# Pooled attention and a GELU MLP on one core: q transposed by DMA, loads reordered, matmuls on zeros added

## The chip, the core and the metric

The kernel runs on one core of a Trainium2 chip. The core has a matrix engine (TensorE, PE in the profile; its weight loads are PEld), a vector engine (VectorE, DVE), an activation engine (ScalarE, ACT), a general engine (GpSimd, POOL) and a queue processor (SyncE, SP). DMAs are issued from SP, ACT or POOL and run on 16 shared DMA engines. PSUM, where matmuls write, has 8 banks of 512 float32 columns on 128 partitions. The metric is the device time of one execution in microseconds (us), as the median of several runs.

## What is computed

Cut to what matters, for q, k and v of shape (8 batches, 8 heads, 576, 64):

```python
k_p = k.reshape(B, H, 72, 8, D).mean(axis=3)      # pooling by 8
v_p = v.reshape(B, H, 72, 8, D).mean(axis=3)
scores = np.matmul(q, k_p.transpose(0, 1, 3, 2)) / np.sqrt(D)
attn = softmax(scores)                            # over the 72 pooled keys
x = np.matmul(attn, v_p)                          # then (B*S, H*D) = (4608, 512)
h = x @ w_in                                      # (4608, 2048)
out = gelu_tanh(h) @ w_out                        # (4608, 512)
```

Inputs and output are float32; the kernel rounds to bfloat16 for the matmuls.

## The kernel before

**Two interleaved streams.** The MLP works through the 4608 tokens in 9 groups of 512 (`GROUP`). Attention works through 8 batches of 576 tokens. Batch 0 is done alone at the start; then group g of the MLP carries the attention of batch g + 1 between its own matmuls. The program order on each engine is written out by hand.

**One batch of attention.** `load_k`, `load_v` and `load_q` bring in float32 rows (q is cast to bfloat16 on the way[...]). k is pooled by three additions on VectorE (`k_steps`, line 135 through `add`), then turned by 5 TensorE transposes (`trans_k`, L162) and copied to `kT` (L168 to L172). v is pooled the same way (`v_steps`), into `vp` (for batch 0 into `vz`). q is turned by 18 TensorE transposes of 128x128 (`trans_q`, L179) into PSUM and copied to `qT` (L184 on ScalarE, L186 on VectorE), in four portions of 5 and 4 blocks (`QG`). Then there are 8 items (2 halves of the columns, 4 head pairs). Per item: `qk` makes two score matmuls (L196), `expo` one exponential (L202), `av` the product with v and the row sums (L215, for batch 0 four matmuls, L220), `norm` the reciprocal of the sums by a logarithm and an exponential on ScalarE (L228 to L233), and `mult` the product on VectorE into `xT` (L241), two instructions of 64 partitions, for batch 0 one of 128.

**One MLP group.** Phase 1: 16 blocks `fo` of 4 matmuls each (`p1_mm`, L266), each block followed by `gelu` on ScalarE (L272). The first four blocks are interleaved, the last `ko` of them last, as they need the latest `xT`. After each block the steps in `side[fo]` are issued, filled from `plan`: the pooling and the transposes of the next batch. Phase 2: 64 matmuls (`p2_mm`, L275); before matmul number `pos` = 6, 14, 20, ... the next batch's `qk`, `av`, `expo` and `norm` are issued, and `mult` some nine matmuls later. Four times per group a finished PSUM bank is copied (L280) and stored from the SP queue (L286).

**Banks.** Phase 1 uses PSUM banks 0 to 3 and 7. `trans_q` uses banks 4 to 7, one per portion, `trans_k` bank 4.

**Queues.** On SP: half of k of batch 0, v of batch 0 in two halves, v of batch 1, later the stores. On ACT: the rest of k of batch 0. On GpSimd: q of batch 0, the four quarters of `w_in`, k and q of batch 1, the four quarters of `w_out`, then at the head of each group g the k, q and v of batch g + 2. These buffers are double, so a load waits until the batch two earlier has been pooled or transposed.

**The start.** After batch 0's k is pooled: two portions of `trans_q`, `trans_k`, two portions of `trans_q`, eight times scores and exponential, `v_steps`, then the eight items of `av`, `norm` and `mult`. 16 matmuls of group 0 on the first 288 columns (`early`) are placed behind items 5, 6 and 7 (`take`). In group 0 the plan is: pooling of v at blocks 1 and 2, of k at block 7, q at 8 to 11, k's transposes at 13. In later groups: k pooled at 2 and 3, q at 4 to 7, k's transposes at 9, v at 10 to 13.

Of the kernel before, what the change touches and what calls it, by code (L numbers as in the profile page):

```python
# [8 lines left out]
F32 = mybir.dt.float32  # L9
BF16 = mybir.dt.bfloat16  # L10
ALU = mybir.AluOpType
# [7 lines left out]
def kernel(  # L19
# [9 lines left out]
    nc = tc.nc  # L29
    B, H, S, D = q.shape  # L30
    Sp = S // 8
# [6 lines left out]
    TP = T // 2  # L38
    CH = S // 2
# [33 lines left out]
    def load_v(b, eng, h0=0, h1=H):  # L73
        if b not in vs:
            vs[b] = kvp.tile([Sp, H, 512], F32, name="vt")
        eng.dma_start(out=vs[b][:, h0:h1],
                      in_=v[b, h0:h1].rearrange("h (j l) d -> j h (l d)", l=8))

    def load_q(b, i0=0, i1=2):
        if b not in qs:  # L80
            qs[b] = qp.tile([128, 2, T * D], BF16, name="qb")
        nc.gpsimd.dma_start(
            out=qs[b][:, i0:i1],
            in_=q[b].rearrange("(i h) (p t) d -> (h p) i (t d)", i=2, t=T)[:, i0:i1])
# [8 lines left out]
    load_k(0, [nc.sync, nc.scalar])  # L93
    load_v(0, nc.sync, 0, 4)
    load_v(0, nc.sync, 4, 8)
    load_v(1, nc.sync)
    load_q(0, 0, 1)
    load_q(0, 1, 2)
    make_identity(nc, identb)
    for i in range(4):  # L100
        nc.gpsimd.dma_start(out=w_in_b[:, :, i * 512:(i + 1) * 512], in_=w_in_v[:, :, i * 512:(i + 1) * 512])


    xT = consts.tile([128, KO, N], BF16, name="xT")
# [5 lines left out]

    vz = consts.tile([Sp, PR, 2, 2, D], BF16, name="vz")
    ones = consts.tile([Sp, 2, 2, D], BF16, name="ones")
    nc.vector.memset(kts[0][0:64, KR], 0.0)
    nc.vector.memset(kps[0], 0.0)
    nc.vector.memset(kTs[0], 0.0)
# [9 lines left out]

    load_k(1, [nc.gpsimd])
    load_q(1)
    for i in range(4):
        nc.gpsimd.dma_start(out=w_out_b[:, 4 * i:4 * i + 4, :], in_=w_out_v[:, 4 * i:4 * i + 4, :])

# [24 lines left out]
    def half_bank(bank):  # L155
        return PS[:, bank, :].bitcast(BF16)

    def trans_k(b, bank, odd_eng=None):
        tp = half_bank(bank)[:, 0:(KR + 1) * 128].rearrange("p (r c) -> p r c", c=128)
        kf = kps[b % 2].rearrange("p r d -> p (r d)")  # L160
        for r in range(KR + 1):
            nc.tensor.transpose(out=tp[:, r, :], in_=kf[:, r * D:r * D + 128], identity=identb)  # L162
        tp = tp[0:D]
        n7 = (H - 1) * KH
        for e in range(2):
            copy = nc.scalar.copy if e and odd_eng is nc.scalar else nc.vector.tensor_copy
            o = kTs[b % 2][e * 64:(e + 1) * 64, e]
            copy(out=o[:, 0:H - 1].rearrange("p h (j r) -> p h j r", r=KR),  # L168
                 in_=tp[:, 0:KR, 0:n7].rearrange("p r (h j) -> p h j r", j=KH))
            copy(out=o[:, H - 1, 0:(128 - n7) * KR].rearrange("p (j r) -> p j r", r=KR),  # L170
                 in_=tp[:, 0:KR, n7:128].rearrange("p r j -> p j r"))
            copy(out=o[:, H - 1, (128 - n7) * KR:], in_=tp[:, KR, 64:128])  # L172

    def trans_q(b, i, t0, n, bank, eng):
        if b not in qTs:
            qTs[b] = bp.tile([128, 2, 4, 32, TP], BF16, name="qT")
        tp = half_bank(bank)[:, 0:n * 128].rearrange("p (t h c) -> p h c t", h=4, c=32)
        for x in range(n):
            nc.tensor.transpose(out=half_bank(bank)[:, x * 128:(x + 1) * 128],  # L179
                                in_=qs[b][:, i, (t0 + x) * 128:(t0 + x + 1) * 128],  # L180
                                identity=identb)
        o = qTs[b][:, i, :, :, t0:t0 + n]
        if eng is nc.scalar:
            nc.scalar.copy(out=o, in_=tp)  # L184
        else:
            nc.vector.tensor_copy(out=o, in_=tp)  # L186

    QG = [(0, 0, 5), (0, 5, 4), (1, 0, 5), (1, 5, 4)]

# [3 lines left out]
    def qk(b, c, pr, bank):  # L193
        for e in range(2):
            h = 2 * pr + e
            nc.tensor.matmul(out=PS[:Sp, bank + e, :CH], lhsT=kTs[b % 2][:, c, h, :],  # L196
                             rhs=qTs[b][:, h // 4, h % 4].rearrange("p c t -> p (c t)"),
                             start=True, stop=True)

    def expo(b, c, pr, bank):  # L200
# [35 lines left out]
    def mult(b, c, pr, bank):  # L236
        rc = rcs.pop((b, c, pr))
        col = b * S + c * CH
        for x in range(2 if b else 1):
            rows = slice(x * 64, (x + 1) * 64) if b else slice(0, 128)  # L240
            nc.vector.tensor_tensor(out=xT[rows, pr, col:col + CH], in0=PS[rows, bank + x, :CH],  # L241
                                    in1=rc[rows], op=ALU.mult)

    ORDER = [(c, pr) for c in range(2) for pr in range(PR)]

# [47 lines left out]
    for s in k_steps(0):  # L293
        s()

    def scores(b, c, pr, bank):
        qk(b, c, pr, bank)
        expo(b, c, pr, bank)

    trans_q(0, *QG[0], 5, nc.scalar)  # L300
    trans_q(0, *QG[1], 6, nc.scalar)
    trans_k(0, 4, nc.scalar)
    trans_q(0, *QG[2], 5, nc.vector)
    trans_q(0, *QG[3], 6, nc.vector)
    for i, (c, pr) in enumerate(((0, 0), (0, 1), (1, 0), (1, 1), (0, 2), (0, 3), (1, 2), (1, 3))):
        scores(0, c, pr, (2, 0)[i % 2])
    for hf in range(2):
        for s in v_steps(0, hf):
# [4 lines left out]
    for i, (c, pr) in enumerate(ORDER):  # L313
        bank = (4, 6, 0, 2, 4, 6, 4, 6)[i]
        av(0, c, pr, bank)
        norm(0, c, pr, bank)
        mult(0, c, pr, bank)
        for fo, ko in early[:take[i]]:
            p1_mm(0, fo, ko, 0, CH)
        early = early[take[i]:]  # L320


    for g in range(NG):
        nb = g + 1 if g + 1 < B else None
        act_set(GELU_SET)
        if g + 2 < B:
            load_k(g + 2, [nc.gpsimd])
            load_q(g + 2)
            load_v(g + 2, nc.gpsimd)


        side = {fo: [] for fo in range(FO)}
        if nb is not None:
            kk = k_steps(nb)
            v0, v1 = v_steps(nb, 0), v_steps(nb, 1)
            tq = [lambda a=a, i=i: trans_q(nb, *a, 4 + i, nc.vector) for i, a in enumerate(QG)]
            tk = [lambda: trans_k(nb, 4)]
            if g:
                plan = {2: kk[:1], 3: kk[1:], 4: tq[:1], 5: tq[1:2], 6: tq[2:3], 7: tq[3:],
                        9: tk, 10: v0[:1], 11: v0[1:], 12: v1[:1], 13: v1[1:]}  # L340
            else:
                plan = {1: v0, 2: v1, 7: kk, 8: tq[:1], 9: tq[1:2], 10: tq[2:3], 11: tq[3:], 13: tk}
            for fo, what in plan.items():
                side[fo] += what

        if g == 0:
            first = [(fo, ko, CH) for ko in range(KO) for fo in range(4)]
        else:  # L350
            late = 3
            rest = [fo for fo in range(4) if fo != late]
            first = [(fo, ko, 0) for ko in range(2) for fo in rest]
            first += [(late, 0, 0), (late, 1, 0)]
            first += [(fo, ko, 0) for ko in (2, 3) for fo in rest + [late]]
        for fo, ko, c0 in first:
            p1_mm(g, fo, ko, c0)
        for fo in range(FO):
            if fo >= 4:
                for ko in range(KO):  # L360
                    p1_mm(g, fo, ko)
            gelu(g, fo)
            for s in side[fo]:
                s()


        todo = {}

        def at(m, f, *a):
            todo.setdefault(m, []).append((f, a))  # L370

        if nb is not None:
            act_set(EXP_SET)
            pos = (6, 14, 20, 27, 34, 41, 48, 55, 61)
            for i in range(len(ORDER) + 1):
                if i < len(ORDER):
                    at(pos[i], qk, nb, *ORDER[i], 2)
                if i:
                    a = (nb, *ORDER[i - 1], 4 + 2 * ((i - 1) % 2))
                    at(pos[i], av, *a)  # L380
                if i < len(ORDER):
                    at(pos[i], expo, nb, *ORDER[i], 2)
                if i:
                    at(pos[i], norm, *a)
                    at(min(pos[i] + 9, 65), mult, *a)
        seq = [(r, fo) for r in range(4) for fo in range(FO)]
        if g == 0:

            seq[:32] = [(r, 4 * f4 + f) for f4 in range(4) for r in range(2) for f in range(4)]
        for m, (r, fo) in enumerate(seq):  # L390
            for f, a in todo.pop(m, []):
                f(*a)
            p2_mm(g, r, fo)
            if fo == FO - 1:
                store(g, r)
        for m in sorted(todo):
            for f, a in todo[m]:
                f(*a)
# [30 lines left out]
```

The softmax here doesn't subtract the row's maximum and nothing guards it: scores larger than these inputs give would overflow.

## Time and profile before

| | |
|---|---|
| median of 5 runs | 320.72 us (319.49 to 322.3) |
| the profiled execution | 319.49 us, of which the span of its instructions is 317.5 us |
| VectorE busy | 176.0 us in 326 instructions |
| ScalarE busy | 222.2 us in 414 instructions |
| L179, q's transposes | 144 instructions, mean 231 ns each |
| L186, copies of q | 15 of 640 columns (mean 820 ns), 15 of 512 (mean 715 ns) |
| L241, `mult`, 64x288 | 112 instructions, mean 455 ns |
| L202, exponential | 64 instructions, mean 643 ns |
| L272, gelu | 144 instructions, mean 602 ns |
| DMA, first 76 us | about 0.25 MB per us |

How to read it: a busy time is the sum over the instructions of an engine. Matmuls overlap each other in the array, so the mean of one is its latency, and what one costs in a row of them is the distance from start to start. "Idle before" is the time in which the engine stood still ahead of an instruction, with what ended it. The chain is followed back from the last instruction through whatever released each step. Two further lines of times are needed below: on VectorE, batch 0's last product (L241) ran from 28.29 to 28.75 us, and the pooling of batch 1's k takes 2.34 us (two additions) and 0.49 us (the third). The `w_in` quarters took a median of 20.6 us from issue to landing, the `w_out` quarters 21.0 us.

### The profile page before, as it was taken

To read this page: it belongs to the slowest core of one execution; us is meant where nothing else is said; L and a number is where in the kernel's file an instruction comes from. 1 tells how busy PE (TensorE), PEld (TensorE's weight loads), DVE (VectorE), ACT (ScalarE), POOL (GpSimd) and SP (SyncE) were. 2 spreads that over 40 slices of the span, in tenths; PEclk is the share of its full clock that TensorE was granted. 3 is DMA by queue.
4 is the path that set the end of the run, shared out by engine and by line. 5 is a ranking of instruction groups with operands and counts; after the bars stand their busy time and mean duration, and the time that the engine had idled before them with its cause. 6 is when DMAs were issued, how large, how long until landed. Compare 5 with 4: busy or idle time off the path is not lost.

```text
span 317.5 us, 4296 instructions
## 1 busy us (share of the span) xinstructions
PE 303.3 (96%) x1624; PEld 156.6 (49%) x1624; DVE 176.0 (55%) x326; ACT 222.2 (70%) x414; POOL 29.5 (9%) x48
## 2 busy tenths in 40 slices
PE   0799999999999999999999999999999999999995
PEld 0556555454555455545554554555555544444442
DVE  2855926677568844984687467755775560010011
ACT  1595679866996789768986898679867987405600
POOL 8512320021002000101011100000000000000000
PEclk9999999999999999999999999999999999999999
DMA  7999999896813562275418440001200210021021
GB/s 230 261 257 263 226 271 208 254 247 160 206 44 132 124 157 94 51 210 125 122 35 223 104 146 34 0 18 51 66 2 0 66 68 0 26 76 34 0 66 66
DMA packets 17113, 37.50 MB, mean 118 GB/s; under 512 B 2021, under 2 KB 6117, under 8 KB 16197
## 3 DMA queue, kind: packets, MB, share of 16 engines
q0 software_dynamic: 10160, 24.26, 33.1%
q1 hardware_dynamic: 6708, 12.32, 12.0%
q10 hardware_dynamic: 224, 0.66, 0.6%
q8 instruction: 12, 0.20, 0.2%
q14 instruction: 9, 0.07, 0.1%
HBM read 36.70 MB, written 9.44 MB: 145 GB/s over the span
## 4 chain that ended last, share of the span: by engine, by line
PE 94%; DMA 2%; DVE 1%; ACT 1%; issue 0%; ACTq 0%; DVEq 0%
PE PS L266 40%; PE PS L275 39%; PE PS L196 5%; PE PS L215 4%; PE PS L220 2%; PE PS L179 2%; DMA kt<-in_k_dram 2%; PE PS L162 1%; DVE kt L135 1%; ACT e L202 1%; DVE osb L280 0%; DVE kT L168 0%; ACT kT L168 0%; DVE kp L135 0%; ACTq L70 0%
## 5 line engine op out<-in xcount | busy, mean ns | idle before, releaser
L275 PE MATMUL PS<-w_out_b,gT 128*128 128x512 bf16 x576 | 136.2, 379 | 0.0
L266 PE MATMUL PS<-xT,w_in_b 128*128 128x512 bf16 (+2 forms) x592 | 134.5, 377 | 0.0
L272 ACT ACTIVATE gT<-PS 128x512 bf16<-128x512 f32 x144 | 81.7, 602 | 52.4 <-PE PS L266 51.6
L266 PEld LDWEIGHTS <-w_in_b 128*128 128x128 bf16 x592 | 57.2, 99 | 60.0 <-issue 1.5
L275 PEld LDWEIGHTS <-gT 128*128 128x128 bf16 x576 | 56.0, 97 | 56.9 <-issue 0.4
L241 DVE TENSOR_TENSOR xT<-PS,rc 64x288 bf16<-64x288 f32 (+1 forms) x120 | 54.6, 455 | 34.5 <-ACT rc L233 26.7
L280 DVE COPY osb<-PS 128x512 f32<-128x512 f32 x36 | 24.9, 691 | 84.0 <-PE PS L275 84.0
L202 ACT ACTIVATE e<-PS 72x576 bf16<-72x576 f32 x64 | 40.8, 643 | 8.4 <-PE PS L196 7.5
L135 DVE TENSOR_TENSOR vt<-vt 72x1024 f32<-72x1024 f32 (+1 forms) x32 | 30.4, 951 | 0.7
L233 ACT ACTIVATE rc<-ld 128x288 f32<-128x288 f32 x64 | 28.3, 443 | 2.0
L196 PE MATMUL PS<-qT,kT 128*72 128x288 bf16 x128 | 27.6, 304 | 0.8 <-ACT e L202 0.8
L228 ACT ACTIVATE ld<-PS 64x288 f32<-64x288 f32 x56 | 22.8, 407 | 1.4
L186 DVE COPY qT<-PS 128x640 bf16<-128x640 bf16 (+1 forms) x30 | 22.0, 768 | 2.7 <-PE PS L179 2.2
L229 ACT ACTIVATE ld<-PS 64x288 f32<-64x288 f32 x56 | 22.5, 402 | 1.4
L247 ACT ACT_TABLE_LOAD x17 | 21.8, 1283 | 2.0 <-issue 1.8
L215 PE MATMUL PS<-e,vp 72*128 72x288 bf16 x112 | 23.1, 285 | 0.0
L179 PE MATMUL PS<-identb,qb 128*128 128x128 bf16 x144 | 13.9, 231 | 9.0 <-DMA qb<-in_q_dram 9.0
L196 PEld LDWEIGHTS <-kT 128*72 128x72 bf16 x128 | 15.1, 119 | 15.0 <-issue 2.1
L135 DVE TENSOR_TENSOR kt<-kt 128x1280 f32<-128x1280 f32 (+1 forms) x16 | 18.5, 1158 | 5.0 <-DMA kt<-in_k_dram 4.6
L179 PEld LDWEIGHTS <-qb 128*128 128x128 bf16 x144 | 11.1, 103 | 16.0 <-DMA qb<-in_q_dram 9.6
L168 DVE COPY kT<-PS 64x504 bf16<-64x504 bf16 x15 | 10.1, 675 | 9.4 <-PE PS L162 9.3
L215 PEld LDWEIGHTS <-vp 72*128 72x128 bf16 x112 | 11.0, 98 | 3.3
(40 smaller groups left out, 77.2 us busy)
## 6 DMA issues: line engine op xcount, KB each, us to landing
kt<-in_k_dram POOLq DMA_DIRECT2D x7, 1024.0 KB, 11.9
vt<-in_v_dram POOLq DMA_DIRECT2D x6, 1152.0 KB, 10.2
out_dram<-osb SPq DMA_DIRECT2D x24, 256.0 KB, 2.0
qb<-in_q_dram POOLq DMA_DIRECT2D x7, 576.0 KB, 12.6
w_in_b<-in_moe_w_in_dram POOLq DMA_DIRECT2D x4, 512.0 KB, 20.6
w_out_b<-in_moe_w_out_dram POOLq DMA_DIRECT2D x4, 512.0 KB, 21.0
out_dram<-osb SPq DMA_DIRECT2D x8, 192.0 KB, 2.2
vt<-in_v_dram SPq DMA_DIRECT2D x2, 576.0 KB
```

The source lines that it names most:

```text
L135: nc.vector.tensor_tensor(out=o, in0=a, in1=b, op=ALU.add)
L179: nc.tensor.transpose(out=half_bank(bank)[:, x * 128:(x + 1) * 128], in_=qs[b][:, i, (t0 + x) * 128:(t0 + x + 1) * 128], identity=identb)
L196: nc.tensor.matmul(out=PS[:Sp, bank + e, :CH], lhsT=kTs[b % 2][:, c, h, :], rhs=qTs[b][:, h // 4, h % 4].rearrange("p c t -> p (c t)"), st ...
L202: nc.scalar.activation(out=e, in_=PS[:Sp, bank:bank + 2, :CH], func=ACT.Exp, scale=1.0 / 64.0)
L215: nc.tensor.matmul(out=PS[:, bank + x, :CH], lhsT=flat(vps[b % 2][:, pr, x]), rhs=e[:, x, :], start=True, stop=True)
L228: nc.scalar.activation(out=ld[0:64], in_=PS[64:128, bank, :CH], func=ACT.Ln)
L233: nc.scalar.activation(out=rc, in_=ld, func=ACT.Exp, scale=-1.0)
L241: nc.vector.tensor_tensor(out=xT[rows, pr, col:col + CH], in0=PS[rows, bank + x, :CH], in1=rc[rows], op=ALU.mult)
L266: nc.tensor.matmul(out=PS[:, h_bank(g, fo), c0:c1], lhsT=w_in_b[:, ko, fo * 128:(fo + 1) * 128], rhs=xT[:, ko, r0 + c0:r0 + c1], start=(ko ...
L272: nc.scalar.activation(out=gTs[g][:, fo, :], in_=PS[:, h_bank(g, fo), :], func=ACT.Gelu_apprx_tanh)
L275: nc.tensor.matmul(out=PS[:, o_bank(g, r), :], lhsT=gTs[g][:, fo, r * 128:(r + 1) * 128], rhs=w_out_b[:, fo, :], start=(fo == 0), stop=(fo ...
L280: nc.vector.tensor_copy(out=osb, in_=PS[:, o_bank(g, r), :])
```

## The change

- q of batches 2 to 7 is no longer transposed by TensorE. At the head of group g (from 1 on) one transposing DMA is issued from SP's queue, from `qb` to `qT`. Batches 0 and 1 keep the TensorE transposes.
- `qT` keeps the order in which a transpose delivers it (block, then 128 columns). The permutation that the copies made is now made by `mult`: it reads PSUM and `rc` with a step and writes `xT` in runs. `qk` reads 9 runs of 32 columns.
- A load of v from SP is split into partitions 0 to 63 and 64 to 71.
- k and q of batch 1 are issued ahead of the second half of `w_in`. v of batch 1 is issued after the fourth item of batch 0, behind a small write by VectorE that makes it wait until then.
- 29 matmuls of 128x512 on zeros (`spin`) are put into batch 0: 16 ahead of the first transposes, 4 and 2 between them, 7 between the score pairs. Nothing reads their result.
- The plan of group 0 is turned round: k pooled at block 0, transposed at 4, q at 6 to 9, v at 10 and 12. In later groups v moves from 10 to 13 to 7, 8, 11 and 12.

```diff
     def load_v(b, eng, h0=0, h1=H):
...
-        eng.dma_start(out=vs[b][:, h0:h1],
-                      in_=v[b, h0:h1].rearrange("h (j l) d -> j h (l d)", l=8))
+        rows = v[b, h0:h1].rearrange("h (j l) d -> j h (l d)", l=8)
+        for j0, j1 in ((0, 64), (64, Sp)) if eng is nc.sync else ((0, Sp),):
+            eng.dma_start(out=vs[b][j0:j1, h0:h1], in_=rows[j0:j1])
...
-    load_v(1, nc.sync)
...
-    for i in range(4):
+    def load_w_in(i):
         nc.gpsimd.dma_start(out=w_in_b[:, :, i * 512:(i + 1) * 512], in_=w_in_v[:, :, i * 512:(i + 1) * 512])
+    load_w_in(0)
+    load_w_in(1)
...
+    idle = consts.tile([128, 512], BF16, name="idle")
+    nc.vector.memset(idle, 0.0)
     nc.vector.memset(kts[0][0:64, KR], 0.0)
...
     load_k(1, [nc.gpsimd])
     load_q(1)
+    load_w_in(2)
+    load_w_in(3)
...
-            qTs[b] = bp.tile([128, 2, 4, 32, TP], BF16, name="qT")
-        tp = half_bank(bank)[:, 0:n * 128].rearrange("p (t h c) -> p h c t", h=4, c=32)
+            qTs[b] = bp.tile([128, 2, TP, 128], BF16, name="qT")
+        tp = half_bank(bank)[:, 0:n * 128].rearrange("p (t c) -> p t c", c=128)
...
-        o = qTs[b][:, i, :, :, t0:t0 + n]
+        o = qTs[b][:, i, t0:t0 + n]
...
+    def trans_q_dma(b):
+        qTs[b] = bp.tile([128, 2, TP, 128], BF16, name="qT")
+        nc.sync.dma_start_transpose(out=qTs[b].rearrange("p i t c -> p (i t) c"),
+                                    in_=qs[b].rearrange("p i c -> p (i c)"))
...
-            nc.tensor.matmul(out=PS[:Sp, bank + e, :CH], lhsT=kTs[b % 2][:, c, h, :],
-                             rhs=qTs[b][:, h // 4, h % 4].rearrange("p c t -> p (c t)"),
+            nc.tensor.matmul(out=PS[:Sp, bank + e, :CH].rearrange("j (t p) -> j t p", p=32),
+                             lhsT=kTs[b % 2][:, c, h, :],
+                             rhs=qTs[b][:, h // 4, :, h % 4 * 32:h % 4 * 32 + 32],
                              start=True, stop=True)
...
-            nc.vector.tensor_tensor(out=xT[rows, pr, col:col + CH], in0=PS[rows, bank + x, :CH],
-                                    in1=rc[rows], op=ALU.mult)
+            nc.vector.tensor_tensor(
+                out=xT[rows, pr, col:col + CH].rearrange("p (c t) -> p c t", t=TP),
+                in0=PS[rows, bank + x, :CH].rearrange("p (t c) -> p c t", t=TP),
+                in1=rc[rows].rearrange("p (t c) -> p c t", t=TP), op=ALU.mult)
...
+    def spin(n):
+        for _ in range(n):
+            nc.tensor.matmul(out=PS[:, 7, :], lhsT=idle[:, 0:128], rhs=idle, start=True, stop=True)
...
+    spin(16)
     trans_q(0, *QG[0], 5, nc.scalar)
     trans_q(0, *QG[1], 6, nc.scalar)
+    spin(4)
     trans_k(0, 4, nc.scalar)
     trans_q(0, *QG[2], 5, nc.vector)
     trans_q(0, *QG[3], 6, nc.vector)
+    spin(2)
     for i, (c, pr) in enumerate(((0, 0), (0, 1), (1, 0), (1, 1), (0, 2), (0, 3), (1, 2), (1, 3))):
+        if i:
+            spin(1)
         scores(0, c, pr, (2, 0)[i % 2])
...
         mult(0, c, pr, bank)
+        if i == 3:
+            vs[1] = kvp.tile([Sp, H, 512], F32, name="vt")
+            nc.vector.memset(vs[1][:, 0, 0:1], 0.0)
+            load_v(1, nc.sync)
...
-            tq = [lambda a=a, i=i: trans_q(nb, *a, 4 + i, nc.vector) for i, a in enumerate(QG)]
+            if g:
+                trans_q_dma(nb)
             tk = [lambda: trans_k(nb, 4)]
             if g:
-                plan = {2: kk[:1], 3: kk[1:], 4: tq[:1], 5: tq[1:2], 6: tq[2:3], 7: tq[3:],
-                        9: tk, 10: v0[:1], 11: v0[1:], 12: v1[:1], 13: v1[1:]}
+                plan = {2: kk[:1], 3: kk[1:], 7: v0[:1], 8: v0[1:], 9: tk, 11: v1[:1], 12: v1[1:]}
             else:
-                plan = {1: v0, 2: v1, 7: kk, 8: tq[:1], 9: tq[1:2], 10: tq[2:3], 11: tq[3:], 13: tk}
+                tq = [lambda a=a, i=i: trans_q(nb, *a, 4 + i, nc.vector) for i, a in enumerate(QG)]
+                plan = {0: kk, 4: tk, 6: tq[:1], 7: tq[1:2], 8: tq[2:3], 9: tq[3:], 10: v0, 12: v1}
```

## The prediction

> **What bounds the kernel now.** I read the page first: engine shares, then the chain that ended last.
>
> ```profile
> PE 303.3 (96%) x1624; PEld 156.6 (49%) x1624; DVE 176.0 (55%) x326; ACT 222.2 (70%) x414; POOL 29.5 (9%) x48
> ...
> PE 94%; DMA 2%; DVE 1%; ACT 1%; issue 0%; ACTq 0%; DVEq 0%
> ```
>
> TensorE is busy for 303.3 of 317.5 us and is 94% of the chain. So a microsecond taken off TensorE's own queue counts in full, and what is taken off ACT or DVE counts only where TensorE waits for it. Two things can therefore be gained: matmuls that needn't be there, and the slow start. Next, TensorE's timeline of batch 2's group, which stands for all groups from 1 to 6:
>
> ```profile
> 93.45 4.74 PE L266 MATMUL PS<-xT,w_in_b 128*128 128x512 bf16 x20
> 98.02 0.44 PE L179 MATMUL PS<-identb,qb 128*128 128x128 bf16 x5
> 98.30 1.03 PE L266 MATMUL PS<-xT,w_in_b 128*128 128x512 bf16 x4
> 99.17 0.39 PE L179 MATMUL PS<-identb,qb 128*128 128x128 bf16 x4
> 99.39 1.03 PE L266 MATMUL PS<-xT,w_in_b 128*128 128x512 bf16 x4
> ...
> 108.80 1.46 PE L275 MATMUL PS<-w_out_b,gT 128*128 128x512 bf16 x6
> 110.10 0.41 PE L196 MATMUL PS<-qT,kT 128*72 128x288 bf16 x2
> ```
>
> Columns: start, time, engine, line. The starts matter, since the ends are modelled: five transposes take 98.30 - 98.02 = 0.28 us of the queue, four take 0.22, so one costs 0.0555 us and not the 231 ns mean of its row. No "idle before" stands anywhere: the queue is full. Last, the start:
>
> ```profile
> 9.03 1.14 PE L179 MATMUL PS<-identb,qb 128*128 128x128 bf16 x9 [9.03 <-DMA qb<-in_q_dram]
> 10.66 0.72 PE L162 MATMUL PS<-identb,kp 128*128 128x128 bf16 x5 [0.48 <-DVE kp L135]
> 11.27 1.14 PE L179 MATMUL PS<-identb,qb 128*128 128x128 bf16 x9
> 12.20 1.17 PE L196 MATMUL PS<-qT,kT 128*72 128x288 bf16 x4
> 13.81 1.18 PE L196 MATMUL PS<-qT,kT 128*72 128x288 bf16 x4 [0.45 <-ACT e L202]
> ...
> 17.53 0.68 PE L220 MATMUL PS<-e,ones 72*128 72x288 bf16 x2
> 18.01 0.68 PE L220 MATMUL PS<-e,vz 72*128 72x288 bf16 x2
> ...
> 27.61 7.39 PE L266 MATMUL PS<-xT,w_in_b 128*128 128x288 bf16 x42
> ```
>
> Here two matmuls of 288 columns start every 0.48 us, 0.24 us each. In the later groups a pair of the same width (110.10 to 110.34, L196) takes 0.12 us each. So all of batch 0's attention runs at half rate, though TensorE has no gap from 17.53 on.
>
> **What the Trainium skill says.** "TensorE: Matmul & The Clock Gate", Part 1, The HAM clock gate: the array idles at half clock and is released after about 3.4 us of sustained activity. The trace agrees on the factor of two (0.24 against 0.12 us), but ten full microseconds of 72-row matmuls (L220) didn't release it; zeros over 128 rows and 512 columns are denser. "DMA: Bandwidth & Descriptors", Why a DMA increments its semaphore by 16: a DMA uses the largest count up to 16 that divides the slowest dimension, so 72 partitions give 12 engines and 64 give 16. No view names the engines, but w_in's quarters landing late beside v fits. "SBUF — State Buffer", Door 1: accesses that change 16-byte line each time are penalised; the trace before has no DVE read of SBUF that changes line with each element.
>
> **Part by part.**
>
> *Transposes (batches 2 to 7).* 6 batches x 18 x 0.0555 = 6.0 us leave TensorE's queue, with nothing in their place; 24 copies on L186 (0.715 to 0.820 us, DVE) go too, worth nothing on an engine at 55%. k's transposes stay. ACT, next in line, does 16 gelus of 0.602 us against TensorE's 16 x 0.863, so it doesn't become the bound. Added is one transposing DMA per group on SP's queue. Queued behind it there are only the stores of the same group, the first of them some 18 us later; ahead of it is the last store of the group before, whose copy L280 ends 0.9 us into the group (126.77 + 0.69 against 126.57). It is due when the first scores matmul needs qT: 110.10 - 93.45 - 1.0 = 15.65 us into the group, so it has 14.7 us. Its cost isn't in the trace. Below: 590 KB at 261 GB/s (the DMA page, Latency and other measured facts) is 2.3 us, an estimate; above: 18 blocks at the 1.309 us that "VectorE: DVE Perf Modes", The three transpose paths, gives for one 128x128 block, 23.6 us. I take 5 to 8 us, since the single block's price must hold a fixed latency: hidden. Its q was loaded a group earlier; in group 1 the queues are still full (0.90 DMA share from 60.3 to 75.7), which may double it, still inside 14.7.
>
> *Layout.* qT now keeps the PE's order, so the scores matmul reads runs of 32 and the permutation moves to L241: PSUM and rc read with a step. For PSUM there is a row: the q copies read it with a step and take 820 - 715 = 105 ns for 128 more elements, 0.82 ns each, no worse than L280's contiguous 691 ns for 512. For rc in SBUF nothing shows it; 0 to twice the 300 ns of 288 elements. I take 0. The cover is thin: the four L241 at the head of a group end at 127.49 + 1.88 = 129.37, and TensorE reaches their data after 12 matmuls, at 126.57 + 2.6 = 129.2.
>
> *Start.* 16 spins need about 16 x 0.43 = 6.8 us at half rate (twice 0.2158, L266's spacing when fast), fewer once released, from about 1.3 us on (behind one more DVE memset), before q lands at 9.03: free. The other 13 stand where TensorE waits anyway (10.2 to 10.66, and 0.20 to 0.45 us per pair for L202). With the fast clock, k's transposes are through 0.3 us earlier, and the eight exponentials run back to back: 12.8 + 8 x 0.593 = 17.55 instead of 18.42. Then each of 8 items costs ACT 0.408 + 0.443 and two gaps of 0.02, 0.89 us, instead of TensorE's 0.96 plus 16 early L266 of 0.24. ACT ends at 17.55 + 8 x 0.89 = 24.7; with 0.2 us for the PSUM banks of the last item and 0.46 for L241, the last product is at 25.4. Before it was 28.29 + 0.46 = 28.75. So 3.35 us are won there.
>
> *Given back.* k_steps(1) now stand directly behind that product on DVE and k's transposes at the end of fo 4. 25.4 + 2.34 + 0.49 = 28.2, but TensorE is done with fo 4 at 25.8 + 0.86 = 26.6: it stalls 1.6 us. From the product on: 2.85 (k_steps) + 0.4 (k's transposes and wait) + 11 x 0.863 + 18 x 0.0555 + 0.3 (bank 4, held by k's copies) = 14.0 us to the first L275; before, 42.31 - 28.75 = 13.56. So 0.45 is given back: net 2.9 us.
>
> *Order of loads.* w_in 2 and 3 come behind 1.8 MB of k and q, but v(1), 1.2 MB, leaves the front. The queues move about 0.25 MB per us until 60 us. My sum puts w_in 2 and 3 at about 27 and 31, due at 31.6 and 35.5; v(1), issued after the fourth product at about 22, at 32, due at fo 10, about 34; the last w_out at 41 (before: 26.58 + 18.6 = 45.2), due at 45.8. All just in time: 0, with up to 2.9 us to lose.
>
> Sum: 6.0 + 2.9 = 8.9 us. The profiled execution took 319.49 (span 317.50 and 1.99 around it), so 310.6 by its own time; it was the fastest of five, 1.23 under their median, so 320.72 - 8.9 = 311.8 by the median.
>
> **Rivals.**
> - A, forecast, 311.8 (309.5 to 313.5): 0.56.
> - B, the clock isn't held. For it: L220's 72 rows never released it, and spins between pairs are few. Against: 16 dense spins. If it falls back in the L220 stretch, the last product is at 27.9: 0.4 instead of 2.9, 314.3. If it never rises, spins of 0.43 us cost about 3 us: 317.7. 0.14.
> - C, slower: the transposing DMA takes more than its 14.7 us. Every microsecond beyond is paid 6 times; from 14.7 + 8.9/6 = 16.2 us on the kernel is slower than before. At 23.6: 311.8 + 6 x 8.9 = 365. For it: the price of a single block; against: 16 engines at 0.45 share or less in groups 2 to 4. 0.08.
> - D, the loads come late and the start's gain goes: 314.7. 0.06.
> - E, L241 at 0.75 us: four at each group's head are 1.2 us late, 7 groups, 8.4 us: 320.2. For it the skill's line, against it the PSUM rows. 0.12.
> - F, no stall at k's transposes and q earlier: 308 to 309.5. 0.04.
>
> **The numbers.** A run of this kernel tells about 0.5% (1.6 us) from nothing: faster is under 319.1, slower over 322.3. Faster: A, B, D, F and a third of E, 0.84; same: half of E, 0.06; slower: C and the rest of E, 0.10. The range: A, D, most of B and the near edge of F, 307.5 to 318, holds about 0.8.
>
> **What would show it.** Groups 2 to 6 at 32.1 us from one L266 x20 to the next instead of 33.1, with no idle before L196; L196 at 0.12 us spacing already at 12 us, L220 too; last batch-0 product near 25.4; L162 of group 0 waiting for DVE kp; the transposing DMA's time to landing under 14 us. Wrong if L196 waits for a DMA, if L241 is above 0.5 us, or if L266 or L275 of group 0 wait for w_in_b or w_out_b.

## The result and the profile after

The changed kernel takes 324.55 us in the median of 27 runs (321.7 to 335.15), against 320.87 us of 48 runs of the kernel before. The ratio is 1.0099, with a 95% interval of 1.008 to 1.0118: it is 1% slower, where 2.8% faster was forecast. (Ratios leave out runs more than 1.5% above the fastest of the same kernel.) The profiled execution took 322.34 us, of which the span is 320.5 us. It is one of the quicker ones: its granted clock (TensorE's clock as a share of the full one) is 0.989 in the mean, and 23 of the 28 runs, the profiled one counted, show 0.984 or less, so most runs spent more time at half clock than the profile below shows.

The page of the changed kernel, in the same parts as before: engine shares, then the chain that ended last by engine and by line. L283 is the former L266, L292 the former L275, L210 the former L196, L256 the former L241.

```profile
PE 301.7 (94%) x1545; PEld 149.8 (47%) x1545; DVE 179.7 (56%) x304; ACT 221.2 (69%) x414; POOL 29.5 (9%) x48
...
PE 75%; DMA 19%; DVE 3%; issue 2%; POOL 1%; POOLq 0%
PE PS L292 37%; PE PS L283 29%; DMA w_out_b<-in_moe_w_out_dram 8%; DMA qT<-qb 7%; DMA w_in_b<-in_moe_w_in_dram 5%; PE PS L230 4%; PE PS L210 4%; DVE xT L256 2%; DVE osb L297 1%; PE PS L171 0%; POOL qb L84 0%; POOL w_out_b L138 0%; POOL w_in_b L103 0%; POOL identb masks.py:199 0%; POOL identb masks.py:197 0%
```

DMA stood for 2% of the chain; it is 19% now, and 7% of the span is a single kind of transfer, `qT<-qb`, the transposing DMA. (The rest is loads of `w_in` and `w_out`; a chain counts the whole of a transfer, but TensorE waited for these only 0.4 and 0.3 us, as shown further below.) The chain in order of time around it (columns: start, duration, what):

```profile
59.98 21.07 DMA qT<-qb
81.05 0.14 issue
81.18 0.67 PE PS L210 x2
81.85 3.29 PE PS L292 x8
```

It is one transfer, that of batch 2, and it took 21.07 us. TensorE's timeline of the same group shows what it cost:

```profile
73.62 1.46 PE L292 MATMUL PS<-w_out_b,gT 128*128 128x512 bf16 x6
81.18 0.67 PE L210 MATMUL PS<-qT,kT 128*72 128x288 bf16 x2 [6.10 <-DMA qT<-qb]
81.64 3.49 PE L292 MATMUL PS<-w_out_b,gT 128*128 128x512 bf16 x8
84.97 0.41 PE L210 MATMUL PS<-qT,kT 128*72 128x288 bf16 x2
```

TensorE stands still for 6.10 us. The eight matmuls behind it then take 3.3 us from start to start of what follows (81.64 to 84.97), where eight of this shape with the fast clock take 1.73: the wait also cost the clock. The view by stretches (PE busy, PEld, DVE, ACT, POOL, then the granted clock, the DMA share and GB/s) agrees, with a clock of 0.50 after the wait:

```profile
76.00:80.00 4.00, 0.00 (x0) 0.00 (x0) 0.00 (x0) 0.00 (x0) 0.00 (x0) 0.76 0.73 219
80.00:84.00 4.00, 2.82 (x8) 1.25 (x9) 0.00 (x0) 0.65 (x1) 1.57 (x2) 0.50 0.26 27
```

Where the 3.0 us of span went, stage by stage, from the first matmul of each phase in both timelines:

| stage | before, us | after, us | difference |
|---|---|---|---|
| start to first L275 / L292 of group 0 | 42.31 | 39.79 | -2.52 |
| second half of group 0 | 18.01 | 18.74 | +0.73 |
| group 1 | 33.13 | 40.94 | +7.81 |
| groups 2 and 3, each | 33.12 | 32.84 | -0.28 |
| groups 4 to 6, each | 32.86 | 32.0 | -0.86 |
| groups 7 and 8, and the end | 59.23 | 59.33 | +0.10 |

One group gives back all that the start and five others win. Groups 2 and 3 win a third of what groups 4 to 6 win. The second reason is in the page's costliest groups, the product on VectorE, 0.644 us in place of 0.455:

```profile
L256 DVE TENSOR_TENSOR xT<-PS,rc 64x288 bf16<-64x288 f32 (+1 forms) x120 | 77.2, 644 | 20.5 <-ACT rc L248 12.8
```

and in TensorE's timeline at the head of group 2, where L283 waits for it:

```profile
99.47 1.89 PE L283 MATMUL PS<-xT,w_in_b 128*128 128x512 bf16 x8
101.73 1.02 PE L283 MATMUL PS<-xT,w_in_b 128*128 128x512 bf16 x4 [0.37 <-DVE xT L256]
103.04 1.24 PE L283 MATMUL PS<-xT,w_in_b 128*128 128x512 bf16 x5 [0.29 <-DVE xT L256]
```

Starts show the gap: eight matmuls need 8 x 0.216 = 1.73 us, the ninth comes after 2.26; four need 0.86, the next comes after 1.31. That is about 1.0 us at each of these heads. The kernel before loses 0.27 us there for the same reason: its ninth and thirteenth L266 start 0.39 and 0.31 us after the one before, and all others 0.216. So about 0.7 us a head is new.

### The profile page after: what moved, and what is told of

Read it like the earlier page. It is cut to its first block, busy times and chain, and to the rows that moved or that the text cites. A ratio compares the mean times of both kernels' runs of the same rounds, so it can differ in the third digit from the quotient of the medians.

```text
span 320.5 us, 4137 instructions
## 1 busy us (share of the span) xinstructions
PE 301.7 (94%) x1545; PEld 149.8 (47%) x1545; DVE 179.7 (56%) x304; ACT 221.2 (69%) x414; POOL 29.5 (9%) x48
## 3 DMA queue, kind: packets, MB, share of 16 engines
q1 hardware_dynamic: 20760, 15.86, 21.2%
## 4 chain that ended last, share of the span: by engine, by line
PE 75%; DMA 19%; DVE 3%; issue 2%; POOL 1%; POOLq 0%
PE PS L292 37%; PE PS L283 29%; DMA w_out_b<-in_moe_w_out_dram 8%; DMA qT<-qb 7%; DMA w_in_b<-in_moe_w_in_dram 5%; PE PS L230 4%; PE PS L210 4%; DVE xT L256 2%; DVE osb L297 1%; PE PS L171 0%; POOL qb L84 0%; POOL w_out_b L138 0%; POOL w_in_b L103 0%; POOL identb masks.py:199 0%; POOL identb masks.py:197 0%
## 5 line engine op out<-in xcount | busy, mean ns | idle before, releaser
L292 PE MATMUL PS<-w_out_b,gT 128*128 128x512 bf16 x576 | 137.9, 382 | 0.1
L283 PE MATMUL PS<-xT,w_in_b 128*128 128x512 bf16 (+2 forms) x592 | 129.8, 373 | 3.0 <-DVE xT L256 2.0
L283 PEld LDWEIGHTS <-w_in_b 128*128 128x128 bf16 x592 | 56.9, 98 | 69.2 <-issue 4.6
L256 DVE TENSOR_TENSOR xT<-PS,rc 64x288 bf16<-64x288 f32 (+1 forms) x120 | 77.2, 644 | 20.5 <-ACT rc L248 12.8
L292 PEld LDWEIGHTS <-gT 128*128 128x128 bf16 x576 | 56.4, 98 | 58.7 <-issue 2.8
L210 PE MATMUL PS<-qT,kT 128*72 128x288 bf16 x128 | 26.4, 288 | 6.2 <-DMA qT<-qb 6.1
L210 PEld LDWEIGHTS <-kT 128*72 128x72 bf16 x128 | 14.5, 114 | 20.8 <-issue 8.4
L230 PE MATMUL PS<-e,vp 72*128 72x288 bf16 x112 | 23.2, 285 | 0.4 <-DVE xT L256 0.4
L230 PEld LDWEIGHTS <-vp 72*128 72x128 bf16 x112 | 11.0, 98 | 3.3
L70 POOL DMA_DIRECT2D kt<-in_k_dram x7 | 4.0, 572 | 90.3 <-DVE kp L144 88.6
L316 PE MATMUL PS<-idle 128*128 128x512 bf16 x29 | 10.4, 485 | 1.2 <-DVE idle L119 1.2
L84 POOL DMA_DIRECT2D qb<-in_q_dram x9 | 6.3, 705 | 23.5 <-DMA qT<-qb 15.2
```

The lines of the kernel that those rows point to most:

```text
L210: nc.tensor.matmul(out=PS[:Sp, bank + e, :CH].rearrange("j (t p) -> j t p", p=32), lhsT=kTs[b % 2][:, c, h, :], rhs=qTs[b][:, h // 4, :, h ...
L230: nc.tensor.matmul(out=PS[:, bank + x, :CH], lhsT=flat(vps[b % 2][:, pr, x]), rhs=e[:, x, :], start=True, stop=True)
L256: nc.vector.tensor_tensor(out=xT[rows, pr, col:col + CH].rearrange("p (c t) -> p c t", t=TP), in0=PS[rows, bank + x, :CH].rearrange("p (t ...
L283: nc.tensor.matmul(out=PS[:, h_bank(g, fo), c0:c1], lhsT=w_in_b[:, ko, fo * 128:(fo + 1) * 128], rhs=xT[:, ko, r0 + c0:r0 + c1], start=(ko ...
L292: nc.tensor.matmul(out=PS[:, o_bank(g, r), :], lhsT=gTs[g][:, fo, r * 128:(r + 1) * 128], rhs=w_out_b[:, fo, :], start=(fo == 0), stop=(fo ...
```

## The experiments

Theory X: the transposing DMA of batch 2 starves, because the 16 DMA engines take turns by packet. Its 256-byte packets then get one turn for each 4 to 8 KB packet of the loads of k and v that fill the queues until about 80 us. The rivals: Y, the slower product and the start cost the time, and the stall would only move; Z, each transposing DMA disturbs its group; X2, the first such DMA is slow for a reason of its own.

### 1. Batch 2's q back on TensorE

```diff
-            if g:
+            if nb > 2:
                 trans_q_dma(nb)
```

(with the plan of before in group 1)

> q of batch 2 alone goes back to the TensorE transposes, with the plan of before in its group; batches 3 to 7 keep the transposing DMA. Theory X (the transposing DMA of batch 2 is starved in full queues: 6.1 us of stall and some 1.7 us at half clock): about 7 us less than the changed kernel (7.8 won, 1.0 given back for 18 transposes), near 317 us, and the other transposing DMAs land in 5 to 7 us. Theory Y (the slower product L256 and the start cost the time, the stall would only move): less than 2 us won. Theory Z (every transposing DMA disturbs its group): no stall in batch 2's group, but another group waits.

Measured: 316.19 us (316.08 to 317.18), ratio to the kernel before 0.9884 (0.9829 to 0.9939), over 8 us less than the changed kernel. In the profile, group 1 takes 33.87 us instead of 40.94. L210 no longer waits for a DMA, and those of the five other transposing DMAs whose landing the trace has take 4.6 to 5.1 us. Y and Z fall as the cause of the loss: nothing moved into another group.

### 2. All six by DMA, the loads of batch 3 held back

```diff
+        if g == 1:
+            trans_q_dma(2)
+            nc.gpsimd.memset(qs[2][:, 0, 0:2], 0.0)
         if g + 2 < B:
             load_k(g + 2, [nc.gpsimd])
...
-            if g:
+            if g > 1:
                 trans_q_dma(nb)
```

The small write goes into `qb`, which the transfer reads, so GpSimd waits for the transfer before it issues the loads.

> All six batches keep the transposing DMA, but the loads of k, q and v of batch 3 are held on GpSimd until the transposing DMA of batch 2 has landed, so that it runs in queues that have drained. Theory X (starved by the loads' large packets): it lands in 5 to 8 us instead of some 20, L210 doesn't wait, near 315 us. Rival X2 (the first transposing DMA is slow by itself, or waits for its q): it still takes over 15 us and the stall stays.

Measured: 315.01 us (314.89 to 315.06), ratio 0.9856 (0.9822 to 0.989). SP's timeline of this kernel shows the issue of batch 2's transfer, beside that of the changed kernel below it (the duration is how long SP was held by handing it out):

```profile
60.61 2.94 SPq L199 DMA_TRANSPOSE qT<-qb  x1
```

```profile
59.98 13.86 SPq L199 DMA_TRANSPOSE qT<-qb  x1
...
100.84 3.82 SPq L199 DMA_TRANSPOSE qT<-qb  x1
```

The same transfer at the same place, now with no load beside it, is handed out in 2.94 us instead of 13.86. It has landed 4.8 us after its issue, when the write that waits for it starts; those of the other five whose landing the trace has take 4.6 to 6.4 us, and L210 doesn't wait. X2 falls.

The single packets in the two traces show how the time divides. q goes out as 2304 packets of 256 bytes. In the changed kernel the first of them starts 4.0 us after the issue, because stores that were handed to SP's queue earlier go ahead of it; the last starts 13.5 us later; then it takes another 3.6 us until the transfer has landed, in which the queue's last 16 packets, of 4 bytes each, go out among the load's packets of 8 KB. With the loads held back the three parts are 1.3, 2.9 and 0.6 us. That SP was slow to hand the transfer out does not explain this: when it had done so, at 73.84 us, 1563 of the packets were still unsent. From 76 to 77 us, when no load packet started, 829 of them went, as many per us as with the loads held back; in the eight us from 66 to 74 it had been 486.

### 3. A spare load put beside a transfer that was fast

On the kernel of experiment 2:

```diff
+        if g == 4:
+            spare = consts.tile([128, 4096], F32, name="spare")
+            rows4 = v[0:4].rearrange("b h s d -> (b h s d)")[0:128 * 8192].rearrange("(p r) -> p r", p=128)
+            nc.scalar.dma_start(out=spare, in_=rows4[:, 0:4096])
```

> The run with held loads, plus one extra load of 2.1 MB (16 KB per partition, into a tile that nothing reads) from ScalarE's queue at the head of group 4, where the queues are otherwise quiet; the store tiles are 4 instead of 6. If the engines take turns by packet, the transposing DMA with its 256-byte packets hardly moves until the extra load is through: it lands in 9 to 12 us instead of 4.7. If they share by bytes: 6 to 8 us. If batch 2's was slow for a reason of its own: 4.7 as in the other groups.

Measured: 320.48 us in a single run, and the transfer of group 4 landed after 17.1 us, with a wait of 3.33 us at L210. So a load alone can make a fast transfer slow, but the size was off by 5 us, and the DMA view says why. Columns of the queue lines: packets, MB, and their time as a share of 16 engines. q1 is SP's queue with the transfer, q0 GpSimd's with the loads. First the changed kernel from 66 to 74 us, where the transfer starved:

```profile
q1 hardware_dynamic: 488, 0.12, 65.8%
q0 software_dynamic: 243, 1.13, 47.9%
```

then this experiment from 160 to 166 us, beside the spare load:

```profile
q10 hardware_dynamic: 118, 1.90, 81.1%
q1 hardware_dynamic: 70, 0.14, 6.1%
```

from 166 to 168 us, with the spare load through and nothing beside the transfer:

```profile
q1 hardware_dynamic: 1706, 0.53, 115.9%
```

and from 168 to 176 us, when the next k load had begun:

```profile
q0 software_dynamic: 169, 1.13, 72.8%
q1 hardware_dynamic: 715, 0.18, 9.9%
```

Alone, q1 sent 1706 packets in 2 us. Beside the loads of the changed kernel it got 488 in 8 us, two for each load packet of 4.7 KB on average (1.13 MB / 243): a tenth of the load's bytes. A sharing by bytes would have moved about as much as the load did, so that is excluded. Strict turns of one packet each would have given one small packet for each large one, so turns by packet are near, but why it is two isn't shown.

In group 4 the spare load did not hold off the transfer itself, but the stores ahead of it in SP's queue: the 70 packets of q1 up to 166 us are of 2 KB each (0.14 MB / 70), and the first 256-byte packet of the transfer starts at 166.2 us. By 168.6 us, 2149 of its 2304 packets had gone. The k load, which ordinarily comes when the transfer is done, then met the last 155, which took until 174.5 us. The forecast of 9 to 12 us had counted the first load only.

### 4. Where the step of the product costs

```diff
-                out=xT[rows, pr, col:col + CH].rearrange("p (c t) -> p c t", t=TP),
-                in0=PS[rows, bank + x, :CH].rearrange("p (t c) -> p c t", t=TP),
-                in1=rc[rows].rearrange("p (t c) -> p c t", t=TP), op=ALU.mult)
+                out=xT[rows, pr, col:col + CH].rearrange("p (c t) -> p t c", t=TP),
+                in0=PS[rows, bank + x, :CH].rearrange("p (t c) -> p t c", t=TP),
+                in1=rc[rows].rearrange("p (t c) -> p t c", t=TP), op=ALU.mult)
```

> The product writes xT with a step instead of reading PSUM and rc with one. If the step on the reads makes the 0.19 us, one product falls from 0.644 to about 0.46 us and the waits of L283 on DVE at the heads of groups 1 to 3 (2.0 us in all, 0.8 more a group than before) go: 2 to 3 us less than the changed kernel, and the batch 2 stall stays. If a step costs the same on the write side, 0.64 us and no change.

Neither came: 408.27 us (403.87 to 409.08). The page of this kernel has the product at 1.433 us, three times its first price, and the waits of TensorE on it add up to some 69 us. Batch 2's stall, which was expected to stay, is gone: group 1 starts so much later that the transfer is issued at 72.32 us, when the loads are nearly through (q0 sends 5 packets from 72 to 76 us), and it is handed out in 2.91 us. That is a second case beside experiment 2, with no load held back.

```profile
L256 DVE TENSOR_TENSOR xT<-PS,rc 64x288 bf16<-64x288 f32 (+1 forms) x120 | 169.9, 1433 | 13.0 <-PE PS L230 5.2
```

The other way, rc written permuted by ScalarE, so that only PSUM is read with a step:

```diff
-        nc.scalar.activation(out=rc, in_=ld, func=ACT.Exp, scale=-1.0)
+        nc.scalar.activation(out=rc.rearrange("p (c t) -> p t c", t=TP),
+                             in_=ld.rearrange("p (t c) -> p t c", t=TP), func=ACT.Exp, scale=-1.0)
...
-                in1=rc[rows].rearrange("p (t c) -> p c t", t=TP), op=ALU.mult)
+                in1=rc[rows].rearrange("p (c t) -> p c t", t=TP), op=ALU.mult)
```

> ScalarE writes rc already permuted, so the product reads rc in runs and only PSUM with a step. If the SBUF read with a step is what costs, the product takes 0.46 us; if the PSUM read does, it stays at 0.64. ScalarE's reciprocal (0.443 us) stays or grows by what its write with a step costs.

The product is back at 0.455 us, so the read of PSUM with a step costs nothing here, and the 0.19 us are the read of rc in SBUF. ScalarE pays for it, 0.720 instead of 0.443 us (two lines of the page's groups):

```profile
L257 DVE TENSOR_TENSOR xT<-PS,rc 64x288 bf16<-64x288 f32 (+1 forms) x120 | 54.6, 455 | 45.7 <-ACT rc L248 42.5
...
L248 ACT ACTIVATE rc<-ld 128x288 f32<-128x288 f32 x64 | 46.1, 720 | 2.0
```

Its one run took 326.64 us, with the stall of batch 2 still in it (8.2 us). Whether it pays was asked of it together with the edit of experiment 1:

> Batch 2's q on TensorE and rc written permuted by ScalarE. The product's 0.19 us then fall on ScalarE as 0.28 us per item. If the waits of L283 at the heads of groups 1 to 3 are the product's price: 2 us less than with batch 2's q on TensorE alone, near 314. If ScalarE's longer item takes their place (batch 0 is bound by it: 8 x 0.28): 2 us back, no difference.

316.24 us (314.98 to 316.5) against 316.19: nothing won. The heads of groups 1 to 3 lose their waits, but the second halves of groups 1 to 6 now take 18.2 us instead of 17.76, because the last two L230 of a group wait for a product that ScalarE's longer items made late: about 0.45 us in each of these six groups.

### 5. The start: alone, without the zeros, with other orders

The edits of the start put into the kernel before, with no transposing DMA and the old layout:

> The kernel before with the changes of the start alone: v in 64 and 8 partitions, the order of loads, the 29 matmuls on zeros, the plan of group 0. q of all batches by TensorE, layout and product as before. By the prediction's sum 2.9 us less than before; by the changed kernel's trace 2.5 us at the first L292 and 0.7 lost again in the second half of group 0: 1.5 to 2.5 us less, near 319.

317.36 us (316.38 to 318.0), ratio 0.9912 (0.9884 to 0.994): 3.4 us won (1.9 to 3.7 by the interval), more than the 1.5 to 2.5 expected; the 2.9 of the prediction lies within. The matmuls on zeros left out of the changed kernel (the diff is `range(n)` to `range(0)` in `spin`):

> The 29 matmuls on zeros left out, all else as changed. If they hold the fast clock: L210 and L235 of batch 0 at 0.24 us spacing again until about 28 us, first L292 some 2.5 us later, near 327 us. If the clock rises without them: no change. If they themselves delay the start: faster than the changed kernel.

330.05 us in the median, 321.37 to 335.98. In its profiled execution (334.22 us) L235 ran at 0.24 us spacing until about 28 us and the first L292 came at 43.1 instead of 39.8, but batch 2's stall was 15.0 us there, so the time of this run can't be read as the zeros' worth. The same with batch 2's q on TensorE:

> As the run with batch 2's q on TensorE, without the 29 matmuls on zeros. If they are worth the fast clock in batch 0: 2 to 3 us more than that run, near 319. If the loads bound the start anyway: no difference.

317.95 us (315.96 to 318.22) against 316.19 (316.08 to 317.18), and the ratios' intervals overlap. Its ten runs form two clusters, two at 315.96 and 316.19 us and eight from 317.56 to 318.22; the profile is of one of the two. In it the fast clock came by itself at about 15 us, and fell back from 21.6 to 25; in the run above, whose start is the same, it came only at 28.4. When it came in the eight isn't shown. With the zeros it came in every one of the eleven profiles within 3.3 to 5.8 us of the first of them, but it did not always hold: in experiment 2, and in six others, it fell back from about 21 us on for 3.4 or 6.8 us, while the changed kernel's own profile held it until the stall of batch 2. So the zeros make the early clock more regular, and their worth, somewhere from nothing to 3 us a run, isn't settled. The two orders, both on the kernel of experiment 2:

```diff
-        for j0, j1 in ((0, 64), (64, Sp)) if eng is nc.sync else ((0, Sp),):
+        for j0, j1 in ((0, Sp),):
```

> The run with held loads, but v of batches 0 and 1 in one piece of 72 partitions from SP. If the split matters (72 rows on fewer engines, which then hold back everything behind): k, q and w_in land later, first L292 1 to 3 us later, 316 to 318. If not: 315.

314.21 us (313.65 to 315.48), ratio 0.9807 (0.9766 to 0.9847): the split of v shows no gain here. And w_in 0 to 3 ahead of k and q of batch 1:

> The run with held loads, but all four quarters of w_in ahead of k and q of batch 1, as before; the plan of group 0 stays turned round, so k of batch 1 is due at block 4. If the order of loads is needed for that plan: k lands about 4 us later, L171 of group 0 waits 2 to 5 us longer, 317 to 320. If not: 315.

318.7 us (316.61 to 320.78), 3.7 more: k's transposes of group 0 wait 6.2 us for the pooling, in place of 1.1, and the clock fell back in that wait, for 6.8 us. The order of the loads is what the turned plan of group 0 rests on.

### 6. A version that beats both

```diff
+    def at_head(b, c, pr):
+        return b in (2, 3) and c == 1 and pr >= 2
...
+            if b < 2:
+                nc.vector.tensor_tensor(out=xT[rows, pr, col:col + CH], in0=PS[rows, bank + x, :CH],
+                                        in1=rc[rows], op=ALU.mult)
+                continue
+            r3 = rc[rows].rearrange("p (c t) -> p c t" if at_head(b, c, pr) else "p (t c) -> p c t", t=TP)
```

(On the kernel of experiment 2. Batches 0 and 1 go back to the old layout, with qT permuted by its copies; where `at_head` holds, ScalarE writes rc permuted. The lines for both are left out here.)

> Built on the run with held loads. The product reads with a step only where that is hidden: batches 0 and 1 keep the old layout of qT (their copies permute), and for the last two items of batches 2 and 3 ScalarE writes rc permuted (0.28 us more each, four times). If the waits of L283 on DVE at the heads of groups 1 to 3 (2.0 us by the profile, about 0.75 us a group against batch groups 4 to 6) are the price of the step: these go and the time falls by 2 to 3 us, to 312 to 313. If they come from the copy L297 ahead of the product: no change from 315.

311.73 us (311.41 to 312.1), ratio 0.9725 (0.9694 to 0.9755). TensorE's timeline of its group 2 shows one unbroken row from the head:

```profile
89.88 9.06 PE L300 MATMUL PS<-xT,w_in_b 128*128 128x512 bf16 x40
98.78 0.44 PE L171 MATMUL PS<-identb,kp 128*128 128x128 bf16 x5
99.06 5.34 PE L300 MATMUL PS<-xT,w_in_b 128*128 128x512 bf16 x24
```

Group 2 takes 32.12 us, from 89.88 to 122.0: the 33.12 of before less 18 transposes, to the hundredth. (The 0.27 us that the kernel before loses at this head are still in it.) In experiment 2 the groups 1 to 3 took 32.87, 32.85 and 32.85 us, so the product's price at the heads is shown: 0.7 us each, 2.2 in all. The other 1.4 us by which this profile is shorter (309.5 against 313.1) come at the start, where the clock fell back in experiment 2 and held here; that they come from the edit is not shown.

## Why the prediction was wrong

*The step that failed* is the cost of the added DMA: "I take 5 to 8 us", and for group 1 the queues "may double it, still inside 14.7". Alone it takes 4.6 to 6.5 us from issue to landing, about as taken. But in group 1 it took 21.07. The doubling is what a sharing by bytes would give, and the prediction gives no other reason for it. The Trainium skill says otherwise, in "DMA: Bandwidth & Descriptors", section Queues, rings and completion order: each engine takes turns between queues "at *packet* granularity". A packet there is a group of descriptors, typically 9 to 17; whether the profile counts the same thing, no run here shows. The trace does show turns rather than bytes, with two of the profile's small packets per large one. The page before could not show the size of these packets. Over the whole run q1 sent 6708 packets then and sends 20760 now: some 2340 more for each of the six transfers (the split of v among them), about 250 bytes each for 590 KB. The question should have been how many turns the transfer needs, and how many large packets are ahead of it. The stores ahead in SP's own queue, which the prediction names, got no time of their own either: with loads beside them, the transfer's first packet came 4.0 us after the issue.

*Rival C* named the place (the transfer later than 14.7 us) and gave it 0.08, but its mechanism, the price of a single block, was wrong: at that price all six would have taken 23.6 us, and five took 4.6 to 6.5. The cost came once. Nor did the prediction price the wait rightly: beside 6.1 us of standing still, 1.6 us went into the half clock after it.

*The product* was taken at no extra cost, with 0 to twice 300 ns as bounds. It measured 0.19 us more, from the SBUF operand, as the passage cited from "SBUF — State Buffer" suggested and the PSUM rows could not exclude. The cover for it was called thin, but by the prediction's own figures there was none: the four L241 end at 129.37 us and TensorE needs them at 129.2. The timeline without an "idle before" hid that the kernel before already waits there, 0.27 us in all. So nearly the whole of the added time was paid at a head, 0.7 us. Rival E counted seven heads; there are three, since from group 4 on a group's tokens no longer reach into the last half of the newest batch (512 x 5 = 2560 tokens end in the first 288 of batch 4).

*The transposes*: 1.0 us per group was right (32.12 against 33.12 where nothing else is changed), hidden in the changed kernel by the product in groups 1 to 3; in groups 4 to 6, 0.86 of it arrived.

*The start*: 2.9 us were forecast and the start alone won 3.4. By its steps in the changed kernel's profile, the 1.6 us stall at k's transposes was 1.16, the eight exponentials ran back to back and ended at 17.5 us, as forecast, the last product ended at 25.24 (forecast 25.4), and the first L292 came at 39.79 (forecast 42.31 - 2.9 = 39.4). Of the loads, w_in made L283 wait only 0.4 us; of the 0.73 us lost in group 0's second half about 0.3 us is a wait for w_out (seven L292 take 1.97 us where 1.67 is their time with the weights there), and 0.38 us is L230 waiting for the slower product. The benefit credited to the split of v doesn't show. Rival B, that the clock falls back, was given 0.14; it happened in seven of the eleven profiles with the zeros. In experiments 1 and 2, where it lasted 3.4 us, the first L292 comes at 40.87 and 40.71 us, and at 38.84 to 39.79 in the three profiles that held the clock through the start (the changed kernel, the start alone, and experiment 6). That the changed kernel's profile held it was luck.

*The sum*: without the two costs it nearly holds. With the stall and the waits at the heads removed the kernel takes 311.73 us, where 311.8 was forecast for a change whose DMA and product cost nothing. That the medians meet to 0.1 us is in part luck: between the profiled executions 8.0 us are won (317.5 to 309.5), not 8.9, of which the transposes give 5.6 (forecast 6.0) and the start with group 0's second half 2.6 (forecast 2.9), less 0.1 at the end.

## What to carry to other kernels

Where other queues are full, price a DMA by its packets and not only by its bytes: here a transfer of 2304 small packets got two of them through for each large packet of the loads, and waited besides for what stood ahead of it in its own queue. Look at the one place where the queues are busy, not at the typical group, and either keep the transfer out of there or hold the others back. When a permutation is moved from one instruction to another, look at which operand takes the step, and at whether someone waits for that instruction. Before calling a clock held, look at more than one profile.

## What the runs showed that was not expected

- What a step costs depended on the operand that takes it. VectorE's product of 64x288 took 0.455 us with PSUM read at 128 bytes' distance, 0.644 with SBUF read so in float32 as well, and 1.433 with bfloat16 written at 18 bytes' distance instead. ScalarE's 128x288 float32 write at 36 bytes' distance took 0.720 instead of 0.443 us.
- From 17.5 to 27.4 us in the kernel before TensorE was busy without a gap, nearly all of it with matmuls on 72 partitions (ten on 128 among them), and its clock did not rise. The zeros, on 128 partitions, raised it in all eleven profiles, 3.3 to 5.8 us after the first one. In eight profiles, one of them without the zeros, the clock fell back between 20.5 and 22.2 us, for 3.4 us in five of them and for 6.8 in three; there stand 72-partition matmuls with waits of about 0.3 to 1.0 us among them. The profiles that held the clock have such waits too, so what decides isn't shown.
- A load with packets of 16 KB nearly stopped the stores in SP's queue: from 160 to 166 us in experiment 3, 70 packets of 2 KB went out beside 118 of the spare load, and the transposing DMA behind them did not begin.
- A transfer isn't done with its last data: in the changed kernel 3.6 of the 6.1 us of TensorE's wait came after the last 256-byte packet.
